# Attention block with a dense Mish layer: maxima ahead of the first scores in groups of three pairs, and other numbers of dense halves in the first and the last steps

## The chip, the core and the metric

The kernel runs on one core of a Trainium2 chip. Its engines are TensorE (PE in the profile; PEld is its weight load), VectorE (DVE), ScalarE (ACT), GpSimd (POOL) and SyncE (SP), which issues the transfers. Each has its own queue and works it off in order; semaphores tie them. The metric is the time of one execution on the device in microseconds (us). The median before is 1700.25 us, of three runs from 1697.17 to 1701.53.

## The reference

The input x is 2048 rows of 512. All arithmetic is float32.

```
mod = (silu(c) @ w_mod) -> six vectors sa, ca, ga, sb, cb, gb
h   = layernorm(x) * (1 + ca) + sa
q, k, v = h @ wqkv, 32 heads of 16
p   = softmax(q k^T / 4);  o = p v
x   = x + ga * (o @ wo)
h   = layernorm(x) * (1 + cb) + sb
u   = h @ w1 + b1                       (1792 columns)
x   = x + gb * ((u * tanh(softplus(u))) @ w2)
```

## The kernel before, in words

**Split numbers.** A dense product is made of three: each operand is split into a rounded high part and a remainder (wh and wl, h_h and h_l, a_h and a_l), and high times high, high times low and low times high are added in one PSUM bank.

**Attention, tiled.** There are 32 iterations n: four blocks of 512 queries by eight groups of four heads. An iteration has 16 steps, one for each 128 keys, so T = 512 steps t. The four heads of a group are two pairs j of two heads s. The tiles `ka` and `qa` hold a pair: one head in rows 0 to 63, the other in rows 64 to 127. A product of one head uses 64 of TensorE's 128 rows, so two products on different halves of the rows run at the same time.

The softmax needs each query's maximum before its scores are made, since the maximum is put as two more rows into `qa`, and the score comes out with it subtracted. So the scores are made twice. Once as *maxima* (`max_tile`: 128 queries by 512 keys in one bank, then VectorE's reduce to one column, L471 and L473), 64 for a pair of heads and 128 for an iteration, 20 steps ahead of the scores (PRO = 20). `neg_max` (L482) reduces them over the key blocks into `mm`, and `max_rows` transposes this to rows (L490), makes their high and low part `mh` and `mt` (L494, L495) and has SyncE put `mt` into `qa` (L501). The second time as *scores*, transposed (128 keys by 512 queries, L512), from which ScalarE makes the exponential `pr` (L520). The *values' product* `pv(t - 2)` (L540) then adds `vg` times `pr` into a bank over the 16 steps; `vg` is loaded for each iteration (L458).

**The banks.** Six of the eight PSUM banks are a ring. A maximum or a score takes the next bank, so each waits until what was there six banks earlier has been read; `ring(2)` takes two neighbours. The other two banks, `ms` and `acc`, take a dense accumulation and the values' product.

**A step from 0 on.** It has four scores, four maxima for the step 20 later (none in the last 20 steps), a values' product, and beside them f *halves* of the dense part: a dense matmul over 64 of its 128 rows, which runs beside a score or a maximum on the other 64. An even step has the halves of the upper rows, the odd step after it those of the lower rows of the same matmuls (`next_part`). f is 8 at most, and 3 in the last 20 steps. [...]

```
            if i < f:
                last = i + 1 == f
...
                if last:
...
                    cur["want"] = True
                    if i < len(mine) and mine[i]:
                        emit(mine[i])
```

`emit` notes the exponential of the next score as `cur["after"]`. With no maxima a step's scores have four slots, i = 0 to 3.

**The prologue.** Steps -20 to -1 have no scores. Each makes four maxima, and then `whole_units` works off whole dense matmuls (all 128 rows), in units of one bank, up to a credit of 7.5, where one is a matmul of 512 columns: 15 matmuls of 256 columns, or 8 of 512. These are the products of the later slices of wqkv (L126), in the order of `plan`; when a unit ends, its results go to memory (`qscr`, `kscr`, `vscr`), from where the pairs are loaded.

**What sets the order.** The program is written out in this order by `step`, and each engine keeps it. `hooks` run at fixed half-steps (2t and 2t + 1): loads, puts, and later stages of a unit. A unit begins when its `ready` time has come. The tail after step T (`tail`) makes the last block's output projection, the down products of the block before that were held, and the last block's dense layer.

Of the kernel before, what the change touches and what calls it, by code (L numbers as in the profile page):

```python
# [8 lines left out]
F32 = mybir.dt.float32  # L9
F32R = mybir.dt.float32r  # L10
AF = mybir.ActivationFunctionType
ALU = mybir.AluOpType
AX = mybir.AxisListType
# [5 lines left out]
def adaln_block(ctx: ExitStack, tc: tile.TileContext, x, wqkv, wo, w1, b1, w2, c, w_mod, out):  # L19
# [20 lines left out]
    CUT1, CUT2 = (0, 1), (2, 3)  # L40
    LOV = ((1,), (), (1, 3), (1, 3))
    PREP = 4
    CREDIT = 7.5
    HCAP = 10.0

    x = x[0]
# [416 lines left out]
    def max_tile(n, j, s, qs, kb):  # L463

        if n not in mxs:
            mxs[n] = ap.tile([P, 2, 8, 4], F32, tag="mx", name="mx", bufs=2)

        def product():
            kt, qt = ka[(2 * n + j) % NR], qa[(2 * n + j) % NR]
            pm = ring()  # L470
            nc.tensor.matmul(pm, qt[64 * s:64 * s + 64, qs * P:(qs + 1) * P], kt[64 * s:64 * s + 64, kb * TB:(kb + 1) * TB],  # L471
                             start=True, stop=True)
            return nc.vector.tensor_reduce(out=mxs[n][:, s, 4 * j + qs, kb:kb + 1], in_=pm, op=ALU.max, axis=AX.X)  # L473

        return product

    def neg_max(n):

        mx = mxs.pop(n)
        mm = ap.tile([P, 4, 2, 4], F32, tag="mm", name="mm", bufs=2)  # L480
        twice = bass.AP(tensor=mx.tensor, offset=mx.offset, ap=[list(mx.ap)[0], [16, 4], [0, 2], [4, 4], [1, 4]])
        nc.vector.tensor_reduce(out=mm, in_=twice, op=ALU.max, axis=AX.X)  # L482
        ats.setdefault(16 * n + 16 - PRO, []).append(lambda: max_rows(n, mm))
# [607 lines left out]
    def queue(ready, make):  # L1091
        units.append((ready, make))
# [4 lines left out]
    def next_part(h):  # L1097

        if not cur["left"] and units and h >= units[0][0]():
            cur["h"] = h  # L1100
            cur["fin"] = units.pop(0)[1]("ms")
            cur["left"], cur["first"] = list(pe_queue), True
            cur.pop("after", None)
            pe_queue.clear()
        slots = []
        for m in cur["left"]:
            if slots and len(slots[-1]) < 2 and m[0].shape[-1] <= TB // 2:
                slots[-1].append(m)
            else:
                slots.append([m])  # L1110
        n = len(slots)
        k = n if n <= 8 else (n + 1) // 2
        if h >= 2 * (T - PRO):
            k = 3
        cur["part"], cur["left"] = slots[:k], [m for l in slots[k:] for m in l]

    def whole_units(h, credit):

        while credit > 0:
            if not cur["left"]:  # L1120
                if not units or h < units[0][0]():
                    return
                cur["tag"] = "acc" if cur.get("tag") == "ms" else "ms"
                cur["h"] = h
                cur["fin"] = units.pop(0)[1](cur["tag"])
                cur["left"] = list(pe_queue)
                pe_queue.clear()
            m = cur["left"].pop(0)
            cur["first"] = False
            mm_go(m)  # L1130
            credit -= m[0].shape[-1] / TB
            if not cur["left"]:
                at(h + 1, lambda fin=cur["fin"]: fin(h + 1))
                cur["fin"] = None
# [7 lines left out]
    def step(t):  # L1142
        second = t % 2
        n, u = t // 16, t % 16 // 2
        tm = t + PRO
        run_hooks(2 * t)
        if t < 0:

            for i in range(2):
                if tm < 16:  # L1150
                    kb, jq = divmod(2 * tm + i, 8)
                else:
                    jq, kb = tm % 16 // 2, 2 * second + i
                for s in range(2):
                    max_tile(tm // 16, jq // 4, s, jq % 4, kb)()
            if second and tm % 16 == 15:
                neg_max(tm // 16)
            run_hooks(2 * t + 1)
            for f in ats.pop(t, []):
                f()  # L1160
            whole_units(2 * t + 1, CREDIT)
            do_specials(2 * t + 1)
            return
        s = 0 if second else 1
        own, others = ([score(n, j, v, 2 * u + i) for i in range(2) for j in range(2)] for v in (s, 1 - s))
        if not second and 1 < t < T:
            next_part(2 * t)
        part = list(cur["part"])
        f = len(part)
        if t >= T:  # L1170
            if t == T:
                cur["tag"] = "acc"
            run_hooks(2 * t + 1)
            pv(t - 2)
            whole_units(2 * t + 1, 8)
            do_specials(2 * t + 1)
            return
        swap, held = False, None
        if tm < T:
            o = max(0, (8 - f) // 2)  # L1180
            mo, alone = maxima(tm // 16, tm % 16 // 2, s, o)

            mine = [x for p in zip(mo, own) for x in p] + own[len(mo):]
            kinds = [k for p in zip("m" * len(mo), "s" * len(mo)) for k in p] + ["s"] * (len(own) - len(mo))
            swap = 2 <= f <= len(mine) and kinds[f - 1] == "s" and kinds[f - 2] == "m"
            if swap:
                mine[f - 2:f] = mine[f - 1], mine[f - 2]
        else:
            o = max(0, (4 - f) // 2)
            mine = own[o:] if second else own[:4 - o]  # L1190
            alone = others[4 - o:] if second else others[:o]

            m = len(mine)
            if f > m:
                mine = [mine[(i * m) // f] if (i + 1) * m // f > i * m // f else None for i in range(f)]
        beside = part + alone

        def emit(product):
            e = product()
            if cur.pop("want", None):  # L1200
                cur["after"] = e

        ends = second and f and not cur["left"]
        for i in range(max(len(mine), len(beside))):
            if i == len(mine) // 2:
                run_hooks(2 * t + 1)
            if i < f:
                last = i + 1 == f
                if i < len(mine) and mine[i] and not last:
                    if swap and ends and i + 2 == f:  # L1210
                        held = mine[i](True)
                    else:
                        emit(mine[i])
                for m in beside[i]:
                    mm_half(m, second, cur["first"], bool(ends and last and m is beside[i][-1]),
                            cur.pop("after", None))
                    cur["first"] = False
                if last:
                    if ends:
                        cur["fin"](2 * t + 2)  # L1220
                        cur["fin"] = None
                    if held:
                        held()
# [3 lines that stand above are left out]
            else:  # L1227
                for x in (*mine[i:i + 1], *beside[i:i + 1]):
                    emit(x)
        if tm < T and tm % 16 == 15:  # L1230
            neg_max(tm // 16)
        do_specials(2 * t + 1)
        pv(t - 2)
        for f in ats.pop(t, []):
            f()
# [13 lines left out]
    def planned(i, a, tag):  # L1249
        _, kind, sl, args = plan[i]  # L1250
        unit = v_unit(sl, a, tag) if kind == 2 else qk_unit(kind, sl, a, tag)

        def fin(h):
            if a == args[-1]:
                if i + 2 < len(plan):
                    d = (7 if i > 6 else 4) if h > 0 else 1
                    at(h + d, lambda: slice_split(*plan[i + 2][1:3]))
                    split_at[i + 2] = h + d
                if i + 3 < len(plan):
                    at(h + (9 if i > 6 else 7 if h > 0 else 2), lambda: slice_load(*plan[i + 3][1:3]))  # L1260
            unit(h)
            if (kind, sl, a) == (2, 0, NKC - 1):
                at(max(0, h + 2), lambda: first_mods(max(0, h + 2)))
            if i + 1 == len(plan) and a == args[-1]:
                mst["qkv"] = h // 2 + 3
        return fin
# [23 lines left out]
        queue_mod(j)  # L1290
    for i, (t0, _, _, args) in enumerate(plan):
        for a in args:
            queue(lambda i=i, t=t0: max(2 * t, split_at.get(i, 4 * T) + 4), lambda tag, i=i, a=a: planned(i, a, tag))

    preps = [(w1scr[f], w1[:, f * P:(f + 1) * P].rearrange("(k p) m -> p k m", p=P), None) for f in range(FT)]
    preps += [(woscr[k], wo[k * P:(k + 1) * P, :], 0) for k in range(DK)]
# [35 lines left out]
    def run_hooks(h):  # L1332
        while h in hooks:
            for f in hooks.pop(h):
                f()
# [37 lines left out]
```

## Time and profile before

| | before |
|---|---|
| median of three runs | 1700.25 us |
| the profiled execution | 1693.26 us |
| its span, first to last instruction | 1691.5 us |
| mean granted clock of TensorE | 0.996 |
| TensorE busy | 1660.6 us, 98% |
| VectorE busy | 1429.9 us, 85% |
| ScalarE busy | 1327.1 us, 78% |
| GpSimd busy | 898.0 us, 53% |
| VectorE's maxima L473, x2048 | 1276.1 us, 684 ns each |
| ScalarE's exponentials L520, x2048 | 1090.2 us, 605 ns each |

Times in the profile are in us from the first instruction, those of one instruction in a group in ns. The chain of waits is the work that ended last, followed back from the end; a row of it is a start, a length, an engine and a line. A timeline row groups instructions of one kind that follow each other, so a group of four matmuls at 0.73 is four that overlap. A matmul's end is modelled, so the distance of two starts tells more than a length.

### The profile page before, as it was taken

The numbers are of one execution on the slowest core, as the hardware profiler recorded it, in microseconds if no ns is written. First come the engines' busy times: TensorE is split into PE (matmuls) and PEld (weight loads), VectorE is DVE, ScalarE is ACT, GpSimd is POOL, SyncE is SP. The second block draws the span as 40 slices with busy tenths as digits, with TensorE's granted clock in tenths as the row PEclk, the third lists the DMA queues.
The fourth block names the chain that finished last, engine by engine and source line by source line (L and its number), as shares of the span: only waits on it lengthen the run. The fifth ranks groups of instructions, "written<-read, shape, count | busy, mean of one in ns | idle before, by whom it ended". The sixth has DMA issues, their size and how long they took to land.

```text
span 1691.5 us, 32962 instructions
## 1 busy us (share of the span) xinstructions
PE 1660.6 (98%) x12316; PEld 921.7 (54%) x12316; DVE 1429.9 (85%) x2362; ACT 1327.1 (78%) x2559; POOL 898.0 (53%) x906
## 2 busy tenths in 40 slices
PE   6999999999999999999999999999999999999998
PEld 5755665554435455555555555555555555554687
DVE  6898898887998888988888888889888888881577
ACT  6247777777778898888889898888888898889264
POOL 5155215565504388755525498654535597646432
PEclk9999999999999999999999999999999999999999
DMA  7767457777772342434353644334442535332362
GB/s 249 192 224 215 120 159 213 250 226 226 232 210 63 111 123 74 127 80 149 86 133 74 197 105 99 99 109 123 117 103 79 176 95 131 93 107 82 132 218 74
DMA packets 113992, 240.03 MB, mean 142 GB/s; under 512 B 24048, under 2 KB 49648, under 8 KB 107784
## 3 DMA queue, kind: packets, MB, share of 16 engines
q1 hardware_dynamic: 113832, 237.92, 49.6%
q8 instruction: 97, 1.59, 0.4%
q14 instruction: 63, 0.52, 0.1%
HBM read 179.95 MB, written 51.44 MB: 137 GB/s over the span
## 4 chain that ended last, share of the span: by engine, by line
PE 92%; DVE 3%; DMA 2%; ACT 2%; SPq 1%; issue 1%; POOL 0%; DVEq 0%; ACTq 0%; POOLq 0%
PE bk L540 30%; PE ring L471 23%; PE ring L512 22%; PE bk L132 9%; PE bk L126 3%; PE ring L126 3%; PE ring L1074 2%; DVE mx L473 1%; ACT pr L520 1%; DMA xt<-in_A_x 1%; SPq L318 0%; DMA qa<-mt 0%; PE bk L1006 0%; DMA vg<-vscr 0%; PE ring L842 0%
## 5 line engine op out<-in xcount | busy, mean ns | idle before, releaser
L473 DVE TENSOR_REDUCE mx<-ring 128x1 f32<-128x512 f32 x2048 | 1276.1, 684 | 161.5 <-PE bk L132 104.9
L520 ACT ACTIVATE pr<-ring 128x512 f32<-128x512 f32 x2048 | 1090.2, 605 | 232.0 <-PE bk L132 168.8
L471 PE MATMUL ring<-ka,qa 64*128 64x512 f32 x2048 | 778.7, 427 | 0.5
L512 PE MATMUL ring<-qa,ka 64*128 64x512 f32 x2048 | 723.0, 397 | 7.8 <-ACT pr L520 4.6
L471 PEld LDWEIGHTS ring<-ka,qa 64*128 64x128 f32 x2048 | 366.5, 184 | 407.9 <-DVE mx L473 356.2
L540 PE MATMUL bk<-pr,vg 128*32 128x512 f32 x4096 | 545.9, 605 | 0.0
L512 PEld LDWEIGHTS ring<-qa,ka 64*128 64x128 f32 x2048 | 374.1, 184 | 120.8 <-ACT pr L520 35.6
L132 PE MATMUL bk<-h,w 64*128 64x512 f32 x1008 | 280.7, 410 | 0.0
L132 PE MATMUL bk<-w,a_h 64*128 64x512 f32 x576 | 194.8, 417 | 0.6 <-ACT pr L520 0.4
L132 PEld LDWEIGHTS bk<-h,w 64*128 64x128 f32 x1008 | 171.5, 184 | 5.7 <-ACT pr L520 0.4
L540 PEld LDWEIGHTS bk<-pr,vg 128*32 128x32 f32 x4096 | 81.0, 108 | 125.1 <-issue 117.0
L740 POOL TENSOR_SCALAR ee<-hb 128x512 f32<-128x512 f32 x42 | 62.5, 1488 | 96.7 <-ACT hb L734 88.2
L132 PE MATMUL bk<-w,a_l 64*128 64x512 f32 x288 | 113.7, 395 | 0.0
L770 POOL TENSOR_TENSOR ee<-ee,rr 128x512 f32<-128x512 f32 x42 | 53.9, 1284 | 111.6 <-ACT rr L761 111.4
L132 PEld LDWEIGHTS bk<-w,a_h 64*128 64x128 f32 x576 | 95.3, 185 | 5.2 <-ACT pr L520 1.5
L132 PE MATMUL bk<-w,o_hl 64*128 64x512 f32 x288 | 79.7, 409 | 0.0
L98 POOL TENSOR_TENSOR a_l<-hb,a_h 128x512 fp32r<-128x512 f32 x53 | 71.7, 1354 | 4.4
L893 POOL TENSOR_TENSOR y<-yd,y 128x512 f32<-128x512 f32 x40 | 51.4, 1285 | 35.5 <-ACT yd L892 35.3
L754 POOL TENSOR_SCALAR rr<-ee 128x512 f32<-128x512 f32 x42 | 26.1, 622 | 60.0 <-ACT ee L746 59.9
L132 PE MATMUL bk<-h_h,wl 64*128 64x512 f32 x168 | 57.5, 423 | 0.0
L95 POOL TENSOR_SCALAR a_h<-hb 128x512 fp32r<-128x512 f32 x53 | 36.3, 684 | 39.9 <-DVE hb L768 38.3
L774 POOL TENSOR_TENSOR hb<-hb,rr 128x512 f32<-128x512 f32 x42 | 54.5, 1298 | 3.3
(205 smaller groups left out, 1840.9 us busy)
## 6 DMA issues: line engine op xcount, KB each, us to landing
ka<-kscr SPq DMA_DIRECT2D x124, 384.0 KB
w<-w2scr SPq DMA_DIRECT2D x56, 512.0 KB
w<-w1scr SPq DMA_DIRECT2D x46, 512.0 KB
vg<-vscr SPq DMA_DIRECT2D x32, 552.0 KB
qa<-qscr SPq DMA_DIRECT2D x124, 100.0 KB
kscr<-qh SPq DMA_DIRECT2D x16, 512.0 KB
qscr<-qh SPq DMA_DIRECT2D x32, 256.0 KB
hl<-in_B_w SPq DMA_DIRECT2D x28, 256.0 KB
```

Source lines behind the costliest of these rows:

```text
L98: (nc.gpsimd if eng == "p" else nc.vector).tensor_sub(lo, src, hi.bitcast(F32))
L126: nc.tensor.matmul(acc, l, r, start=start, stop=stop)
L132: i = nc.tensor.matmul(acc, l[64 * g:64 * g + 64], r[64 * g:64 * g + 64], start=start, stop=stop)
L471: nc.tensor.matmul(pm, qt[64 * s:64 * s + 64, qs * P:(qs + 1) * P], kt[64 * s:64 * s + 64, kb * TB:(kb + 1) * TB], start=True, stop=True)
L473: return nc.vector.tensor_reduce(out=mxs[n][:, s, 4 * j + qs, kb:kb + 1], in_=pm, op=ALU.max, axis=AX.X)
L512: nc.tensor.matmul(p_, kt[64 * s:64 * s + 64, kc * P:(kc + 1) * P], qt[64 * s:64 * s + 64, :], start=True, stop=True)
L520: e = nc.scalar.activation(pr, p_, AF.Exp, scale=SCALE)
L540: nc.tensor.matmul(accs[n][32 * h:32 * h + 32, :], vgs[n][:, o:o + 32], pts.pop((t, h)), start=(kc == 0), stop=(kc == 15))
L740: nc.gpsimd.tensor_scalar_min(buf("ee", 2), b["hb"], HCAP)
L770: nc.gpsimd.tensor_mul(ee, ee, rr)
L774: nc.gpsimd.tensor_mul(hb, hb, rr)
L893: nc.gpsimd.tensor_add(y[i], yd, y[i])
```

## The change

**Prologue.** The maxima are made in groups of three pairs. A pair is the two heads' product for the same queries and keys; `max_pair` writes both into two neighbouring banks of the ring and reduces both with one instruction, 128x2 out of 128x2x512. A group stands in every third half-step, followed by whole dense matmuls up to a credit of 3 x 3.6 = 10.8: 22 of 256 columns or 11 of 512. Forty pairs are thirteen groups and one pair alone, which has a credit of 1. `neg_max(0)` stands right after pair 31 and `max_rows(0)` after pairs 33 to 35, ahead of the dense matmuls of that step. The prologue has four dense matmuls of 512 columns fewer than before, and the steps from 0 on have them as eight halves.

**First steps.** The halves begin with step 0 instead of step 2: f was 0, 0, 8, 8, 6, 6 and so on, and is 6 from step 0 on.

**Last 20 steps.** The largest number of halves is 4 instead of 3. f was 3 in each; it is 4, 4, 2, 2, then twelve times 4, then four times 0. The first half of a step after one with f = 4 waits for the exponential of the fourth score.

**Split slices.** A unit whose weight slice is split in the prologue may begin one half-step after the split rather than four.

From step 4 to step 491 TensorE, VectorE, ScalarE and GpSimd have the same instructions in the same order.

```diff
-    CREDIT = 7.5
+    CREDIT = 3.6
...
+    def max_pair(n, j, qs, kb):
+
+        if n not in mxs:
+            mxs[n] = ap.tile([P, 2, 8, 4], F32, tag="mx", name="mx", bufs=2)
+        kt, qt = ka[(2 * n + j) % NR], qa[(2 * n + j) % NR]
+        pm = ring(2)
+        for s in range(2):
+            nc.tensor.matmul(pm[:, s, :], qt[64 * s:64 * s + 64, qs * P:(qs + 1) * P],
+                             kt[64 * s:64 * s + 64, kb * TB:(kb + 1) * TB], start=True, stop=True)
+        nc.vector.tensor_reduce(out=mxs[n][:, :, 4 * j + qs, kb], in_=pm, op=ALU.max, axis=AX.X)
...
         if h >= 2 * (T - PRO):
-            k = 3
+            k = 4
...
         if t < 0:
 
             for i in range(2):
-                if tm < 16:
-                    kb, jq = divmod(2 * tm + i, 8)
-                else:
-                    jq, kb = tm % 16 // 2, 2 * second + i
-                for s in range(2):
-                    max_tile(tm // 16, jq // 4, s, jq % 4, kb)()
-            if second and tm % 16 == 15:
-                neg_max(tm // 16)
-            run_hooks(2 * t + 1)
-            for f in ats.pop(t, []):
-                f()
-            whole_units(2 * t + 1, CREDIT)
+                run_hooks(2 * t + i)
+                pairs = [p for p in range(2 * tm + i, min(2 * tm + i + 3, 2 * PRO)) if (2 * tm + i) % 3 == 0]
+                for p in pairs:
+                    kb, jq = divmod(p, 8) if p < 32 else (p % 4, p % 32 // 4)
+                    max_pair(p // 32, jq // 4, jq % 4, kb)
+                    if p % 32 == 31:
+                        neg_max(p // 32)
+                if i:
+                    for f in ats.pop(t, []):
+                        f()
+                if pairs:
+                    whole_units(2 * t + i, 3 * CREDIT if len(pairs) == 3 else 1)
             do_specials(2 * t + 1)
             return
...
-        if not second and 1 < t < T:
+        if not second and t < T:
             next_part(2 * t)
...
-            queue(lambda i=i, t=t0: max(2 * t, split_at.get(i, 4 * T) + 4), lambda tag, i=i, a=a: planned(i, a, tag))
+            queue(lambda i=i, t=t0: max(2 * t, split_at.get(i, 4 * T) + (4 if split_at.get(i, 0) > 0 else 1)), lambda tag, i=i, a=a: planned(i, a, tag))
```

The order that comes of it is shown at four places. A row has the line, the operation, out<-in and the shape. Lines from L477 on are 11 higher after the change.

TensorE in the prologue, from one set of maxima to the next. Before:

```order
L471 MATMUL ring<-ka_104,qa_106 128x512 x4
L126 MATMUL bk<-wh,h_h 128x256 x4
L126 MATMUL bk<-wl,h_h 128x256 x4
L126 MATMUL bk<-wh,h_l 128x256 x4
L126 MATMUL bk<-wh,h_h 128x256 x3
L471 MATMUL ring<-ka_104,qa_106 128x512 x4
```

And after:

```order
L484 MATMUL ring<-ka_104,qa_106 128x512 x6
L126 MATMUL bk<-wh,h_h 128x256 x4
L126 MATMUL bk<-wl,h_h 128x256 x4
L126 MATMUL bk<-wh,h_l 128x256 x4
L126 MATMUL bk<-wh,h_h 128x256 x4
L126 MATMUL bk<-wl,h_h 128x256 x4
L126 MATMUL bk<-wh,h_l 128x256 x2
L484 MATMUL ring<-ka_104,qa_106 128x512 x2
L484 MATMUL ring<-ka_105,qa_107 128x512 x4
```

Four maxima to 15 dense matmuls became six to 22.

VectorE's queue of maxima over the prologue and into the first steps. Before:

```order
L473 TENSOR_REDUCE mx<-ring 128x1 x64
L482 TENSOR_REDUCE mm<-mx 128x32
L473 TENSOR_REDUCE mx<-ring 128x1 x4
L494 TENSOR_SCALAR mh<-ring 32x128
L495 SCALAR_TENSOR_TENSOR mt<-mh,lows,ring 32x128
L473 TENSOR_REDUCE mx<-ring 128x1 x60
```

And after:

```order
L486 TENSOR_REDUCE mx<-ring 128x2 x32
L493 TENSOR_REDUCE mm<-mx 128x32
L486 TENSOR_REDUCE mx<-ring 128x2 x4
L505 TENSOR_SCALAR mh<-ring 32x128
L506 SCALAR_TENSOR_TENSOR mt<-mh,lows,ring 32x128
L486 TENSOR_REDUCE mx<-ring 128x2 x4
L473 TENSOR_REDUCE mx<-ring 128x1 x48
```

Sixty-four reduces of a bank became thirty-two of two banks; between mm and mh stand four pairs (eight banks) instead of four banks.

SyncE's queue around the puts of the maxima's rows into `qa` (`wr` is a raw slice of wqkv, `ql` and `qh` are the parts of a finished q or k unit). Before:

```order
L501 DMA qa_106<-mt 2x4x128 x2
L501 DMA qa_107<-mt 2x4x128 x2
L458 DMA vg<-vscr 128x1104
L214 DMA wr<-in_A_wqkv 128x4x256
L252 DMA qscr<-ql 8x16x512
L252 DMA qscr<-qh 8x16x512 x2
```

And after:

```order
L512 DMA qa_106<-mt 2x4x128 x2
L512 DMA qa_107<-mt 2x4x128 x2
L214 DMA wr<-in_A_wqkv 128x4x256
L252 DMA qscr<-ql 8x16x512
L252 DMA qscr<-qh 8x16x512 x2
L458 DMA vg<-vscr 128x1104
```

The load of `vg` moved behind the load of `wr` and three puts.

TensorE in the last 20 steps, one step, with the wait that stands on a dense half (`Activation_49` is ScalarE's semaphore). Before:

```order
L512 MATMUL ring<-qa_108,ka_633 128x512
L132 MATMUL bk<-w_16036,a_h 128x512 [waits Activation_49]
L512 MATMUL ring<-qa_109,ka_634 128x512
L132 MATMUL bk<-w_16036,a_h 128x512
L132 MATMUL bk<-w_16036,a_l 128x512
L512 MATMUL ring<-qa_108,ka_633 128x512
L512 MATMUL ring<-qa_109,ka_634 128x512
L540 MATMUL bk<-pr_2_1177,vg 32x512
```

And after:

```order
L523 MATMUL ring<-qa_108,ka_633 128x512
L132 MATMUL bk<-w_16861,a_l 128x512 [waits Activation_49]
L523 MATMUL ring<-qa_109,ka_634 128x512
L132 MATMUL bk<-w_16896,a_h 128x512
L523 MATMUL ring<-qa_108,ka_633 128x512
L132 MATMUL bk<-w_16896,a_h 128x512
L132 MATMUL bk<-w_16896,a_l 128x512
L523 MATMUL ring<-qa_109,ka_634 128x512
L551 MATMUL bk<-pr_0_1140,vg 32x512
```

A fourth half stands ahead of the fourth score, and the wait of the next step's first half is on that score's exponential.

## The prediction

> **What bounds the kernel now.** I read the page first (its span, engines, chain by engine, costliest groups), then the chain of waits at both ends of the program, since the change leaves the middle as it is, then the timelines there.
>
> ```profile
> span 1691.5 us, 32962 instructions
> PE 1660.6 (98%) x12316; PEld 921.7 (54%) x12316; DVE 1429.9 (85%) x2362; ACT 1327.1 (78%) x2559; POOL 898.0 (53%) x906
> PE 92%; DVE 3%; DMA 2%; ACT 2%; SPq 1%; issue 1%; POOL 0%; DVEq 0%; ACTq 0%; POOLq 0%
> L473 DVE TENSOR_REDUCE mx<-ring 128x1 f32<-128x512 f32 x2048 | 1276.1, 684 | 161.5 <-PE bk L132 104.9
> ```
>
> TensorE carries 92% of the chain, VectorE 3%, ScalarE 2%. From step 4 to step 491 the four compute engines have the same work in the same order in both programs, so I take no difference there. What is left is about 60 us at the start and 45 us at the end. The chain at the start (start, duration, what):
>
> ```profile
> 50.16 0.66 PE ring L471 x3
> ...
> 53.88 1.08 PE ring L471 x4
> ...
> 56.94 0.66 PE ring L471 x4
> 57.61 1.99 PE bk L126 x15
> ...
> 80.85 0.66 PE ring L471 x4
> 81.51 2.04 PE bk L126 x8
> ...
> 91.67 0.47 PE ring L471 x2
> 92.14 2.48 DVE mx L473 x4
> 94.65 0.29 DVE mm L482
> ...
> 97.89 12.57 DVE mx L473 x21
> 110.50 0.50 PE ring L512
> ...
> 111.23 1.00 PE bk L540 x8
> ...
> 114.43 1.00 PE bk L540 x8
> ...
> 117.26 0.99 PE bk L540 x8
> ```
>
> Until 91.67 it is TensorE alone: a prologue step is four maxima (0.66) and then whole dense matmuls, 1.99 for fifteen of 256 columns or 2.04 for eight of 512, so 2.65 or 2.70. From 92.14 to 110.5 VectorE is the chain: its maxima, back to back at 12.57/21 = 0.60, are late, and the first scores stand in the same ring of banks behind them. From 111.23 it is TensorE again.
>
> The first two steps took 3.72 and 3.06; 1.48 over two of 2.65. The row of that stretch has a granted clock of 0.66 (the number ahead of the DMA share), and 1.00 in the next stretches, so I leave these 1.48 as they are:
>
> ```profile
> 50.00:55.00 5.00, 5.00 (x25) 3.75 (x25) 3.44 (x6) 1.48 (x3) 1.28 (x1) 0.66 0.58 205
> ```
>
> **The prologue's new price.** The parts, from the timeline:
>
> ```profile
> 58.36 0.64 PE L126 MATMUL bk<-wh,h_h 128*128 128x256 f32 x4
> 78.08 0.73 PE L471 MATMUL ring<-ka,qa 64*128 64x512 f32 x4
> 78.61 2.48 DVE L473 TENSOR_REDUCE mx<-ring 128x1 f32<-128x512 f32 x4
> 79.08 1.09 PE L126 MATMUL bk<-h_h,wl 128*128 128x512 f32 x4
> ```
>
> A 256-column matmul starts every 0.12 (2.0 for fifteen, with 0.19 for the first), a 512-column one every 0.23 (2.04 = 8 x 0.23 + 0.20), a maximum of a head every 0.115 after the first ((0.73 - 0.39)/3, a lone one taking 0.39), since two heads run on the two halves of the rows. A reduce starts 0.53 after its matmuls do and takes 0.62.
>
> After the change, a group of three pairs on TensorE is 0.66 + 2 x 0.115 = 0.89, then 22 matmuls of 256 (22 x 0.12 + 0.19 = 2.83) or 11 of 512 (11 x 0.23 + 0.20 = 2.73): 3.72 or 3.62, where one and a half steps were 3.98 or 4.05. Pairs 0 to 29 are ten groups; the 144 narrow matmuls fill 6.5 of them, so 6.5 x 3.72 + 3.5 x 3.62 = 36.9. The group that holds pairs 30 to 32 starts at 50.16 + 1.48 + 36.9 = 88.5; before, pairs 30 and 31 started at 91.67. That is 3.2 us gained, if VectorE keeps up.
>
> The reduce of a pair, 128x2x512, is not in the trace. Its lower bound: the single at 0.60 plus 512 more elements at the slope between the single (684 ns mean, 512 elements) and mm (0.29, 128 elements), (684-290)/384 = 1.03 ns each, 0.53: 1.13. Upper bound: two of the group's mean, 1.37; two back to back are 1.20 to 1.24. I take 1.14, nearest to the slope, since the fixed part should be paid once. Three are then 3.42, under the 3.62 of a group, and TensorE stays the bound. [...]
>
> After the groups, VectorE's order decides. Reduce of pair 30 from 89.0, 31 to 91.3, mm 0.29 (94.65 row), 32 to 92.7, 33 to 93.9. The transposes of the maxima need pair 33's two banks (the ring of six is full), so TensorE, with the dense matmuls queued behind them, stands still for about 1.1 until 93.9. Pairs 34 and 35 to 96.1, mh and mt about 0.6 to 96.7; pairs 36 to 38 from 97.2 to 100.65, the last pair to 102.0. Then nine singles of 0.60, the last nine of the 21 in the 12.57 row, to 107.4, where before it was 110.46: 3.0 gained. The halves that now stand in steps 0 and 1 lie under these reduces (a step of four singles is 2.4; TensorE's part of such a step without the values' product is 2.83 - 1.00 = 1.8). Step 3 has six halves instead of eight: 114.43 - 111.23 = 3.20 becomes 117.26 - 114.43 = 2.83, 0.37 gained. Fewer instructions on VectorE (40 fewer) are worth nothing elsewhere.
>
> SyncE's queue: the four puts of the maxima's rows now come two loads and three puts earlier than the load of vg.
>
> ```profile
> 99.23 3.07 SPq L501 DMA_DIRECT2D qa<-mt  x4
> 102.35 0.39 SPq L458 DMA_DIRECT2D vg<-vscr  x1
> ...
> 104.48 1.55 SPq L252 DMA_DIRECT2D qscr<-qh  x2
> ```
> ```profile
> 104.30 0.50 PE L512 MATMUL ring<-qa,ka 64*128 64x512 f32 x1
> ```
>
> The rows took 104.30 - 102.30 = 2.0 at most from the last issue to the first score. After the change mt is ready near 96.7 and the puts end near 100.3 or earlier, so the first score can start by 102.3, when TensorE arrives at about 101.5; VectorE has its backlog until 102.0 and on, which covers that. The vg load, before at 102.35, goes behind the qscr puts, in the times of before to 104.48 + 1.55 - 0.39 = 105.6; with mt about 2 us earlier I put it at 103.6. Its first reader, the values' product (111.23 before), now wants it at 108.2. Before, its landing was hidden in 8.9 us; now 4.6 are left. The nearest transfer I can see, the rows' 2.0, fits; vg is larger, so I add 0.2. Prologue: -3.0 - 0.37 + 0.2 = **-3.2**; with the pair reduce at 1.24 it is -2, and if the standstill of 1.1 goes too, -4.5.
>
> **The end.** Without maxima a step is four scores, four exponentials, three halves (now four, for fourteen of the steps) and a values' product.
>
> ```profile
> 1526.64 0.50 PE L512 MATMUL ring<-qa,ka 64*128 64x512 f32 x1
> ...
> 1549.24 0.50 PE L512 MATMUL ring<-qa,ka 64*128 64x512 f32 x1
> 1549.29 0.50 PE L132 MATMUL bk<-w,a_h 64*128 64x512 f32 x1
> ...
> 1551.36 0.50 PE L512 MATMUL ring<-qa,ka 64*128 64x512 f32 x1
> 1551.92 0.49 PE L132 MATMUL bk<-w,a_h 64*128 64x512 f32 x1
> ...
> 1553.81 0.49 PE L512 MATMUL ring<-qa,ka 64*128 64x512 f32 x1
> ...
> 1569.77 2.78 PE L540 MATMUL bk<-pr,vg 128*32 128x512 f32 x24
> ```
> ```profile
> 1549.77 1.08 ACT pr L520 x2
> 1550.86 0.52 ACT rr L761
> 1551.38 0.50 ACT pr L520
> ```
> ```profile
> 1555.79 15.45 ACT L520 ACTIVATE pr<-ring 128x512 f32<-128x512 f32 x29
> ```
>
> The first two steps shown are an ordinary one (1549.24 to 1551.36, 2.12) and one that waits (to 1553.81, 2.45). The wait is on a rule in the code: a step's first half is held until the exponential of the score written at the last slot of the step before has ended. With three halves that is the third exponential. It starts 0.53 after the step's first score (1549.77 - 1549.24) at the earliest, each takes 15.45/29 = 0.53 (0.52 where ACT is pressed), so the third ends at 0.53 + 1.58 = 2.11, and the next step's half is due at 2.12 + 0.05 = 2.17: no wait, unless ScalarE has one more operation between, as at 1550.86; then the half starts 0.04 after the third exponential (1551.92) and the next step 1.89 later (1553.81).
>
> With four halves the last slot's score is the fourth, whose exponential ends at 0.53 + 2.10 = 2.63. The half is held from 2.17 to 2.67, the next three scores stand behind it in TensorE's order, and the step that starts after it comes 1.89 + 0.23 (the fourth half, in a row of halves that nothing hides now) = 2.12 later, at 4.79. By then ScalarE has just ended that step's exponentials and starts anew: two steps take 4.7 to 4.8 instead of 4.24, 0.46 to 0.55 more, and there are seven such pairs: 3.2 to 3.9. I walked all twenty steps by these durations with the extra ScalarE operations in their places. The walk of before gives 43.6 to 43.9 for 44.13 in the trace (1526.64 to 1569.77 + 1.0) and its long steps; that of after ends its last exponential 3.7 later. One exponential of the last mish unit (0.5) that stood behind the last score now stands ahead of six; it is in that walk. Before, three products of values (2.78) end the stretch; now one or two are left, 0.3 back. **+3.3.** The bounds: +0.3 if the held half never costs anything, +5 if ScalarE's extra operations all add to it.
>
> Nothing comes back for the dense part's earlier end:
>
> ```profile
> 1584.65 1.29 POOL L98 TENSOR_TENSOR a_l<-hb,a_h 128x512 fp32r<-128x512 f32 x1
> ...
> 1598.62 0.71 PE L126 MATMUL ring<-w,a_h 128*128 128x512 f32 x2
> ```
>
> The last unit's output is ready at 1585.9, and the tail's products on the later blocks run from 1598.62; the units it feeds come after. The four last steps have no halves, but ScalarE's four exponentials still take 2.1 each.
>
> **Sum.** -3.2 + 3.3 = +0.1. The profiled execution took 1693.26 (span 1691.5), under the 1700.25 that is the median of the runs; I carry the difference over to the median: 1700.4.
>
> **The rivals.** (B) The held half costs little, because the order on the chip lets ScalarE run ahead: then 1700.25 - 3.2 + 0.3 = 1697.3, and with the prologue's better bound 1696.1; with an end that gains its 0.3 and more from the dense part's early finish it is under 1695. For it: an ordinary step of three halves has no wait; against it: the step at 1551.36, which waits in just this way. (C) Slower: the pair reduce costs two of the mean, 1.37. Then three are 4.11, VectorE is the bound of each group (4.11 against 3.7, ten groups: +4) and pairs 30 to 39 cost 0.23 more each (+2.3): 1700.4 + 6 = 1706.4. It decides from 1.33 on, where the sum passes 0.3%. Against it: the back-to-back singles of 0.60. (D) The values' product waits for vg: it decides at 4.6 us from issue to landing, and the worst, the 8.9 that the trace allows, gives 1700.4 + 4.3 = 1704.7. (E) The pair reduce costs two singles back to back, 2.48/2 = 1.24: three take 3.72, TensorE and VectorE run level in each group, and pairs 30 to 39 cost 0.10 more each: 1701.4. [...] That the change does less than it says (the pairs not back to back) is within C and E.
>
> **How the numbers follow.** Two runs of this kernel tell about 0.3% apart, 5.1 us: 1695.2 to 1705.3. Both parts cancelling, 1697 to 1704: 0.50. B 0.17, of which most with something more gained at the end, under 1695.2. C with other ways for the prologue to lose 0.15, D 0.10, E 0.08. The two ends of D's and A's range put a few hundredths over the line. Faster 0.19, same 0.55, slower 0.26. The range takes B's and C's nearer halves: 1694.5 to 1706.5.
>
> **What would show it.** In the profile after: groups of 0.89 and 22 or 11 dense matmuls every 3.6 to 3.7 until about 88.5; the pair reduce at 1.14, three in a row without idle TensorE; the first values' product near 108; from 1523 on steps alternating 2.1 and 2.6; the last exponential within 0.5 us of 1571.2 (1555.79 + 15.45). A pair reduce over 1.25, a stop of TensorE before its first values' product, or last steps all of 2.12, would make it wrong.

## The result and the profile after

The changed kernel takes 1708.03 us (median of 7 runs, 1704.15 to 1710.56), the kernel before 1697.32 (7 runs, 1691.92 to 1701.53): slower by a ratio of 1.0061, 95% interval 1.0047 to 1.0075. That is 10.7 us by the medians, 0.6%, and 1.5 us over the predicted range. The page of the changed kernel begins:

```profile
span 1708.8 us, 32922 instructions
```

The reduce to `mm` is done once an iteration, after its 64 maxima (2048 in 32 iterations; the 128 named with the kernel is wrong), at the same place in both programs, and so serves as a milestone. Its timeline rows after (first, second and last of 32; start, duration):

```profile
93.67 0.29 DVE L493 TENSOR_REDUCE mm<-mx 128x32 f32<-128x128 f32 x1
147.81 0.29 DVE L493 TENSOR_REDUCE mm<-mx 128x32 f32<-128x128 f32 x1
1541.73 0.29 DVE L493 TENSOR_REDUCE mm<-mx 128x32 f32<-128x128 f32 x1
```

and the second and the last of before:

```profile
139.70 0.29 DVE L482 TENSOR_REDUCE mm<-mx 128x32 f32<-128x128 f32 x1
1526.88 0.29 DVE L482 TENSOR_REDUCE mm<-mx 128x32 f32<-128x128 f32 x1
```

The first stands 1.0 us earlier than before (94.65), the second 8.1 later, the last 14.9 later, the end of the span 17.3 later. So 9.1 us are lost between 94 and 148 us, 2.4 behind the last milestone, and 6.7 in the middle. Of the middle's, 5.1 are in TensorE's waits for the maxima's rows of later iterations, from 130 to 1600 us (total, times, longest); after:

```profile
PE ring L523 <- DMA qa<-mt: 7.6, 3, 4.2
```

and before:

```profile
PE ring L512 <- DMA qa<-mt: 2.5, 1, 2.5
```

These waits differ between profiles whose middle has the same work: 4.7 in one of the kernel before with only its last 20 steps changed (e5 below), 4.0 in one with the groups of three (e6). The profile of before is also a low one of its kernel, 1693.26 for a median of 1697, and that of the changed kernel the longest of its seven, 1710.56. So the two profiles differ by more than the medians; start and end, 8.1 + 2.4 = 10.5, are about the size of the 10.7.

**The start.** The chain after, in the prologue:

```profile
52.24 4.99 PE bk L126 x22
...
61.35 0.89 PE ring L484 x6
62.24 2.83 PE bk L126 x22
65.07 0.89 PE ring L484 x6
...
83.53 0.90 PE ring L484 x6
...
87.13 0.94 PE ring L484 x6
...
90.81 0.94 PE ring L484 x6
```

The groups run as reckoned, 0.89 and 2.83, 3.72 in all (61.35 to 65.07), later 3.60. But pair 30's group starts at 90.81, 2.3 later than forecast. SyncE's queue and TensorE's timeline around the first scores (a number in brackets is idle time and what ended it):

```profile
95.32 0.80 SPq L303 DMA_DIRECT2D ka<-kscr  x2
98.25 0.39 SPq L214 DMA_DIRECT2D wr<-in_A_wqkv  x1
...
99.77 2.98 SPq L512 DMA_DIRECT2D qa<-mt  x4
105.82 0.39 SPq L214 DMA_DIRECT2D wr<-in_A_wqkv  x1
...
108.43 1.64 SPq L458 DMA_DIRECT2D vg<-vscr  x1
```
```profile
105.93 0.79 PE L523 MATMUL ring<-qa,ka 64*128 64x512 f32 x1 [1.82 <-DMA qa<-mt]
...
116.91 1.94 PE L551 MATMUL bk<-pr,vg 128*32 128x512 f32 x8 [3.32 <-DMA vg<-vscr]
...
122.06 1.47 PE L551 MATMUL bk<-pr,vg 128*32 128x512 f32 x8
```

The first score waits 1.82 us for the maxima's rows, issued only 0.5 us later than before (99.77 against 99.23). The first values' product waits 3.32 us for vg: 108.43 is 6.1 later than before, because the wr load ahead of it could not be issued before wr was free, at 105.82, and it then took 8.5 us to the product. What held wr is in the chain: the slice in it landed 5.50 us after its issue, and only then could ScalarE and GpSimd split it, until 105.80 (start, length):

```profile
98.25 5.50 DMA wr<-in_A_wqkv
...
104.53 1.27 POOL wl L98
```

Behind each stop the granted clock (the number ahead of the DMA share) is low, 0.66 and then 0.61 and 0.71:

```profile
105.00:110.00 5.00, 4.07 (x19) 2.94 (x21) 2.34 (x5) 2.48 (x6) 2.66 (x3) 0.66 0.50 145
...
115.00:120.00 5.00, 3.09 (x14) 1.24 (x16) 0.39 (x1) 0.00 (x0) 1.63 (x1) 0.61 0.92 332
120.00:125.00 5.00, 5.00 (x32) 2.65 (x30) 3.29 (x6) 3.55 (x7) 4.76 (x5) 0.71 0.07 28
```

So the product of the second step starts 122.06 - 116.91 = 5.15 after the first, where before it was 114.43 - 111.23 = 3.20. Of the 8.1 us, 5.7 stand at the first values' product (116.91 against 111.23) and nearly all of the rest by the second.

**The end.** TensorE's and ScalarE's timelines in two of the last steps:

```profile
1571.50 0.49 PE L523 MATMUL ring<-qa,ka 64*128 64x512 f32 x1
...
1573.67 0.50 PE L523 MATMUL ring<-qa,ka 64*128 64x512 f32 x1
1574.14 0.49 PE L132 MATMUL bk<-h,w 64*128 64x512 f32 x1
...
1576.26 0.49 PE L523 MATMUL ring<-qa,ka 64*128 64x512 f32 x1
...
1587.05 4.07 PE L551 MATMUL bk<-pr,vg 128*32 128x512 f32 x24
```
```profile
1572.03 4.24 ACT L531 ACTIVATE pr<-ring 128x512 f32<-128x512 f32 x8 [0.53 <-PE ring L523]
```

One step (1571.50 to 1573.67) waits for nothing and takes 2.17, the next holds its half for 0.47 and takes 2.59: 4.76 for two instead of 4.24. ScalarE, which should be the bound here, idles 0.53 us in every eight exponentials. From the last `mm` to the end of the last values' products it is 45.7 us before (1526.88 to 1569.77 + 2.78) and 49.4 after (1541.73 to 1587.05 + 4.07), 3.7 more. The end of the span shows only 2.4 because 1.3 come back in the tail: both traces have a stop of TensorE of 2.42 us there (until 1604.08 and 1622.64), behind which the granted clock is 0.72 before (1605 to 1610) and 1.00 after (1620 to 1630). The tail behind the products takes 119.0 us in before and in e3, which has four halves, and 117.7 in the changed kernel and in e5, so this is a difference of executions, not of the change.

### The profile page after: what moved, and what is told of

Read it like the earlier page. It is cut to its first block, busy times and chain, and to the rows that moved or that the text cites. A ratio compares the mean times of both kernels' runs of the same rounds, so it can differ in the third digit from the quotient of the medians.

```text
span 1708.8 us, 32922 instructions
## 1 busy us (share of the span) xinstructions
PE 1665.0 (97%) x12320; PEld 924.8 (54%) x12320; DVE 1427.1 (84%) x2322; ACT 1326.7 (78%) x2559; POOL 897.5 (53%) x906
## 3 DMA queue, kind: packets, MB, share of 16 engines
q1 hardware_dynamic: 113832, 237.92, 49.4%
## 4 chain that ended last, share of the span: by engine, by line
PE 89%; DMA 3%; ACT 2%; DVE 2%; POOL 2%; issue 1%; SPq 0%; DVEq 0%; POOLq 0%; ACTq 0%
PE bk L551 29%; PE ring L471 22%; PE ring L523 21%; PE bk L132 9%; PE bk L126 3%; PE ring L126 2%; ACT pr L531 2%; PE ring L1085 2%; DMA qa<-mt 1%; PE ring L484 1%; DMA wma<-in_w_mod 1%; DVE mx L473 0%; DMA wm<-in_w_mod 0%; POOL wm L634 0%; DVE hf L374 0%
## 5 line engine op out<-in xcount | busy, mean ns | idle before, releaser
L473 DVE TENSOR_REDUCE mx<-ring 128x1 f32<-128x512 f32 x1968 | 1227.4, 684 | 174.3 <-PE bk L132 119.6
L471 PE MATMUL ring<-ka,qa 64*128 64x512 f32 x1968 | 764.4, 427 | 0.0
L471 PEld LDWEIGHTS ring<-ka,qa 64*128 64x128 f32 x1968 | 361.6, 185 | 402.8 <-DVE mx L473 350.9
L98 POOL TENSOR_TENSOR wl<-wr,wh 128x512 fp32r<-128x512 f32 (+1 forms) x13 | 17.7, 1365 | 75.9 <-ACT wh L91 43.6
```

The costliest lines, as they stand in the source:

```text
L98: (nc.gpsimd if eng == "p" else nc.vector).tensor_sub(lo, src, hi.bitcast(F32))
```

## The experiments

The theories: A, the held half costs the end 2 to 4 us; B, vg and the rows of the maxima are late because of their places in SyncE's queue; against B, C, the transfers of 95 to 115 us are too many in any order. A median is given with that of before from runs made beside it; a ratio is to before, with its 95% interval.

**e1, three halves again.**

```diff
         if h >= 2 * (T - PRO):
-            k = 4
+            k = 3
```

> The changed kernel with three halves in each of the last 20 steps again, nothing else undone. The traces put +8.1 us on the start and +2.4 on the end (the offset of the second reduce to mm is 8.1, that of the span 17.3, of which 14.8 stand ahead of the last 20 steps). Theory A, the held half of a step costs the end 2.4 to 3.3: this kernel is 2.4 to 3.3 us faster than the changed kernel, about 8 us slower than before, and its last 20 steps are 2.12 each again. Rival, the end's difference is only carried over from the start: the same time as the changed kernel, within 0.5 us.

Measured: 1704.24 us, before 1697.41, ratio 1.0045 (1.0029 to 1.0061). The difference to before falls from 10.7 to 6.8 us, by 3.9; the intervals of the two kernels overlap, so it is the profile, and e5 below, that decide. A holds for the end: its last steps run without a wait, and the offset to before stays the same from the last milestone on (10.7 there, 10.6 at the span's end). The first scores and the first values' product wait as in the changed kernel.

**e2, vg back at its place.**

```diff
-    at(-3, lambda: load_v(0))
+    at(-4, lambda: load_v(0))
```

> The changed kernel with the load of vg directly behind the maxima's rows, where it stood before; the other transfers keep the new order. Theory B, the place of vg in SyncE's queue costs the 3.75 us for which TensorE waited for it and the lower granted clock after that stop: the first values' product has no wait for vg, starts near 113.5 instead of 116.9, and the time falls by 5 to 6 us to about 1702. Rival C, the transfers of 95 to 115 us are too many for the DMA engines in whatever order: the product still waits for vg, or the first scores wait longer for the rows, and less than 2 us are won.

Measured: 1703.62 us, before 1697.41, ratio 1.0043 (1.0022 to 1.0065); 4.5 us of the 10.7 are gone by the medians, though the two intervals overlap. vg is not waited for, but in the profiled execution the first scores wait longer for their rows:

```profile
108.37 0.79 PE L523 MATMUL ring<-qa,ka 64*128 64x512 f32 x1 [5.02 <-DMA qa<-mt]
...
116.64 1.06 PE L551 MATMUL bk<-pr,vg 128*32 128x512 f32 x8
```

So vg's place is worth most of what B expected, and part of C is seen: the product came no earlier (116.64), only the stop and the low clock behind it are gone (1.00 over 115 to 120 us, in the changed kernel 0.61).

**e3, vg and the load of the fourth pair back.** As e2, and

```diff
-    for pp, h in ((2, -22), (3, -8)):
+    for pp, h in ((2, -22), (3, -10)):
```

> As the kernel with vg back, and the load of the fourth pair of q and k ahead of the last kscr puts, where it stood before: SyncE's queue is that of before around the first scores. Theory B with the fourth pair's 0.9 MB in the way of the maxima's rows: the rows land 2 us after their issue instead of 3.2, the first scores start near 104 instead of 105.9, and the time falls by 7 to 8 us to about 1700, with the end's 2.4 left over. Rival, the rows are late because mt is late (four pair reduces between mm and mh instead of four single ones, mt at 99.0 against 97.9): the first scores still wait 1 us or more, and it is within 1 us of the kernel with vg back alone.

Measured: 1698.95 us, before 1697.41, ratio 1.0013 (1.0003 to 1.0024). Another 4.7 us are gone, as B expected, and within 1.5 us of before although the end still has four halves. The first score still waits, but shorter, and the values' product starts at 111.86:

```profile
105.11 0.50 PE L523 MATMUL ring<-qa,ka 64*128 64x512 f32 x1 [1.65 <-DMA qa<-mt]
...
111.86 1.07 PE L551 MATMUL bk<-pr,vg 128*32 128x512 f32 x8
```

**e4, the kernel before with vg late.**

```diff
-    at(-3, lambda: load_v(0))
+    at(-1, lambda: load_v(0))
```

> The kernel before with the load of vg behind the load of wr and the three qscr puts, as in the changed kernel; nothing else. It prices that place alone. Theory B: vg is issued near 106.0, lands 6 to 8 us later, the first values' product moves from 111.2 to about 113 or 114, the granted clock falls after the stop, and the kernel is 3 to 6 us slower than before. Rival, vg is late in the changed kernel only because its queue waited for a free wr: issued at 106.0 it is there by 111.2 and the time is that of before within 1 us.

Measured: 1703.13 us, before 1697.41, ratio 1.0039 (1.0024 to 1.0053): this place alone costs 5.7 us. SyncE's row and TensorE's:

```profile
109.47 1.29 SPq L458 DMA_DIRECT2D vg<-vscr  x1
```
```profile
117.68 1.94 PE L540 MATMUL bk<-pr,vg 128*32 128x512 f32 x8 [5.15 <-DMA vg<-vscr]
```

The rival falls: vg needs 8.2 us from its issue, and was issued 3.5 us later than I put it, since the wr loads ahead of it waited for their buffers here too (the first went out at 100.27, 2.6 later than before, with mt only 0.1 later).

**e5, the kernel before with four halves.**

```diff
-            k = 3
+            k = 4
```

> The kernel before with four halves in a step of the last 20, the start untouched. Theory A: the end costs 2.4 to 3.9 us (2.4 by the spans of the two traces, 3.8 between the changed kernel and the one with three halves), so it is that much slower than before, and its last 20 steps alternate 2.1 and 2.6. Rival, the end costs this only behind a disturbed start: within 1 us of before.

Measured: 1700.33 us, before 1697.06, ratio 1.0024 (1.0012 to 1.0035), 3.3 us. A holds without a disturbed start: ScalarE's rows have the same gap,

```profile
1566.14 4.24 ACT L520 ACTIVATE pr<-ring 128x512 f32<-128x512 f32 x8 [0.54 <-PE ring L512]
```

**e6, SyncE's order of before and three halves.** e3 and e1 together; of the change there remain the groups of three pairs, the halves from step 0 and the earlier unit after a split.

> The changed kernel with SyncE's order of before (vg and the fourth pair back) and three halves in the last 20 steps: what is left are the groups of three pairs and the halves from step 0. The kernel with SyncE's order back was 1.5 us slower than before, 2.4 to 3.9 of it the end's: so 1 to 2.4 us faster than before. Rival, the groups themselves gain nothing, since the rows of the maxima come no earlier (mt behind four pair reduces) and the first scores wait for them: the time of before within 0.5 us.

Measured: 1696.28 us, before 1697.06, ratio 0.9998 (0.9986 to 1.0009). No difference: the rival. Where the groups' gain goes is seen against the profile of e5, whose start is that of before. e6, then e5 (first maxima, where the first group stops, first values' product):

```profile
52.08 0.97 PE L484 MATMUL ring<-ka,qa 64*128 64x512 f32 x5
53.59 0.49 PE L484 MATMUL ring<-ka,qa 64*128 64x512 f32 x1 [0.54 <-DVE ql L98]
54.01 0.75 PE L126 MATMUL bk<-wh,h_h 128*128 128x256 f32 x4
...
104.76 0.49 PE L523 MATMUL ring<-qa,ka 64*128 64x512 f32 x1 [1.38 <-DMA qa<-mt]
...
111.41 1.06 PE L551 MATMUL bk<-pr,vg 128*32 128x512 f32 x8
```
```profile
49.85 0.73 PE L471 MATMUL ring<-ka,qa 64*128 64x512 f32 x4
50.52 0.75 PE L126 MATMUL bk<-wh,h_h 128*128 128x256 f32 x4
...
110.30 1.07 PE L540 MATMUL bk<-pr,vg 128*32 128x512 f32 x8
```

The first group takes 54.01 - 52.08 = 1.93 to its dense matmuls instead of 0.89: it needs all six banks, and the sixth is held by a set-up unit until VectorE has made its ql. (The later start itself, 52.08 against 49.85, stands ahead of the first maximum.) The product comes 59.33 us after the first maximum, in e5 60.45. So 1.1 us of the forecast 3.2 are left there in these two profiles; 1.0 went at the first group and 1.4 in the wait for the rows. Even the 1.1 is no more than starts differ by: in e8, whose maxima are those of before, the product comes 59.60 after the first. SyncE had mt's puts behind a wr load that went out at 99.79, 1.5 after mt.

**e7, the rows ahead of wr.** As e6, with the puts of the first rows right behind mt and the wr load behind them.

```diff
-        at(2 * (16 * n + 16 - PRO) + 3, put)
+        put() if n == 0 else at(2 * (16 * n + 16 - PRO) + 3, put)
...
-                    at(h + (9 if i > 6 else 7 if h > 0 else 2), lambda: slice_load(*plan[i + 3][1:3]))
+                    x = h + (9 if i > 6 else 7 if h > 0 else 2)
+                    at(-6 if -10 < x < -4 else x, lambda: slice_load(*plan[i + 3][1:3]))
```

> As the kernel with SyncE's order of before and three halves, but the four puts of the first maxima's rows go straight behind mt, ahead of the load of wr, which in the profiles held SyncE until wr was free (100.15 with the order back) while mt was ready. Theory D, the first scores wait because the rows' puts stand behind a load that waits for its buffer: the wait of 1.65 us is gone and it is 1 to 2 us faster than the kernel with the order back. Rival, the rows are late by the transfers that run at the time, or mt is: no change within 0.7 us, or a loss, where the later wr delays the weights of the next dense unit.

Measured: 1699.66 us, before 1697.06, ratio 1.0017 (1.0003 to 1.0031). The wait for the rows is gone from the profile, and the values' product starts at 113.24, later than in e6. The rival holds, by another way than it says: wr now comes later, ScalarE stands still for it with the first exponentials behind that in its queue (they start at 106.67, in e6 at 105.29), and TensorE waits 1.08 us for them. Behind that its scores and maxima start 0.43 us apart (109.01, 109.44, 109.87), later 0.23 (117.40, 117.63, 117.86). ScalarE, then TensorE:

```profile
105.66 0.62 ACT L91 CAST wh<-wr 128x512 fp32r<-128x512 f32 x1 [4.58 <-DMA wr<-in_A_wqkv]
...
106.67 3.67 ACT L531 ACTIVATE pr<-ring 128x512 f32<-128x512 f32 x7
```
```profile
104.51 0.39 PE L523 MATMUL ring<-qa,ka 64*128 64x512 f32 x1
...
113.24 1.07 PE L551 MATMUL bk<-pr,vg 128*32 128x512 f32 x8
```

**e8, the kernel before with the rows ahead of wr.** The first edit of e7 in before.

> The kernel before with only the puts of the first maxima's rows moved ahead of the load of wr and one unit's kscr puts. In the profile of before the first scores did not wait for the rows, in that of the same kernel with a late vg they waited 1.2 us. Theory D: 0 to 1.5 us faster than before, according to how often the wait occurs. Rival: the rows' early transfer changes nothing, within 0.5 us.

Measured: 1698.88 us, before 1697.06, ratio 1.0010 (0.9994 to 1.0026). Nothing won.

**e9 and e12, two pairs in the first group.** As e6, with groups of 2, twelve times 3, and 2 pairs.

```diff
-                pairs = [p for p in range(2 * tm + i, min(2 * tm + i + 3, 2 * PRO)) if (2 * tm + i) % 3 == 0]
+                q = 2 * tm + i
+                pairs = list(range(q, min(q + 3, 2 * PRO))) if q % 3 == 2 else [0, 1] if q == 0 else []
...
-                    whole_units(2 * t + i, 3 * CREDIT if len(pairs) == 3 else 1)
+                    whole_units(2 * t + i, len(pairs) * CREDIT if q < 38 else 4.6)
```

> As the kernel with SyncE's order of before and three halves (0.8 us under before), but the groups of pairs are 2, then twelve of 3, then 2. In the profiles the first group of three needs all six banks of the ring, one of which a set-up unit holds until VectorE has made its ql: the sixth maximum stops TensorE (0.54 us idle, 2.2 from the group's start to its dense matmuls instead of 0.9). And mt stands behind four pair reduces, with these groups behind three. Theory E: the stop at the start is gone (1.0 to 1.3 us), mt comes another 1.2 us earlier, the first scores wait less for their rows: 1.5 to 3 us faster than the kernel with three in the first group, so 2 to 4 us faster than before. Rival: what is won at the start the first scores give back, because their rows land when the transfers of 95 to 105 us let them: within 0.7 us of the kernel with three.

> The kernel with two pairs in the first group once more, beside the one with early puts: 1.7 us under before as in the run before, give or take 1.5.

Measured: 1694.81 us, before 1696.50, ratio 0.9991 (0.9979 to 1.0004); once more 1697.00, before 1696.48, ratio 0.9997 (0.9985 to 1.0009). The first group's stop is gone, and mt is ready at 95.52, in e6 at 98.28 (1.8 of these 2.8 us stand ahead of the first maximum, 50.31 here). The rows are put only 0.4 earlier, and the first score waits 1.44:

```profile
95.18 0.34 DVE L506 SCALAR_TENSOR_TENSOR mt<-mh,lows,ring 32x128 fp32r<-32x128 f32 x1
```
```profile
99.39 0.38 SPq L214 DMA_DIRECT2D wr<-in_A_wqkv  x1
...
100.90 3.02 SPq L512 DMA_DIRECT2D qa<-mt  x4
```

Theory E falls by the time. What VectorE and TensorE win ahead of the rows ends at SyncE, which issues the puts 5.4 us after mt, behind a wr load that waits for its buffer. TensorE also stops for 1.52 us, until 99.41 (1.07 in e12, 1.66 in e11), for the low part of a weight slice that GpSimd makes from wr.

**e11, both.** e9 with the first edit of e7.

> As the kernel with two pairs in the first group, but the first maxima's rows are put into qa straight behind mt. In the profile of that kernel mt was ready at 95.5 and its puts were issued from 100.9, behind a wr load that SyncE could issue only at 99.4; the first scores waited 1.4 us for the rows. Theory D: the wait goes, 1 to 1.4 us faster than with the late puts. Rival, as in the two runs that put the rows first before (2.6 and 1.8 us over before): wr and vg come later by as much, and the time is the same or up to 3 us longer.

Measured: 1697.24 us, before 1696.48, ratio 0.9998 (0.9985 to 1.0011). The rows go out at 99.43, the first score at 105.19 waits for none, and the values' product starts at 112.33, against 110.97 in e9; from the first maximum it is 60.24 against 60.66, so most of the wait won is lost again (TensorE waits 0.74 us for ScalarE's exponentials, as in e7). No version of the groups was clearly faster than before.

**e10, the loads behind vg later.** The changed kernel, with the two wm loads that follow vg ten half-steps later.

```diff
-                at(max(0, h + 2), lambda: first_mods(max(0, h + 2)))
+                at(max(0, h + 2) + 10, lambda: first_mods(max(0, h + 2) + 10))
```

> The changed kernel with the loads of w_mod's slices (wm, 0.5 MB each), which follow vg at once in SyncE's queue, ten half-steps later; they shift what follows them in the middle of the program, so the time is only to be read at the start. In the changed kernel vg was issued at 108.4 to 110.1 and waited for until 116.9. Theory B, the place in the queue: vg comes at most 1 us earlier. Rival C, the wm transfers slow vg: it lands 2 to 4 us earlier, and the first values' product starts by 114.5.

Measured: 1709.70 us (two runs), before 1696.50, ratio 1.0073 (1.0044 to 1.0102). vg was issued at 110.17 and its reader started at 119.65, 9.5 us later, so vg is slow without the wm loads right behind it:

```profile
119.65 1.31 PE L551 MATMUL bk<-pr,vg 128*32 128x512 f32 x8 [3.25 <-DMA vg<-vscr]
```

This bears on the cause as well. In the changed kernel the chain from 98 to 151 us runs through wr, SyncE, a wm load (110.12, 8.18 us) and GpSimd's work on it, not through vg; here, with wm later, it runs through wr and vg. Both stand behind the same wr load.

## Why the prediction was wrong

**Where the 10.7 us come from**, taken off one after the other: vg's place 4.5 (e2; alone in before 5.7, e4), the fourth pair's place 4.7 (e3), the fourth half 2.3 (e6 against e3; 3.9 and 3.3 in e1 and e5). By the ratios it is 3.1, 5.1 and 2.5. Clear of noise are the two loads together (e3), vg's place alone (e4) and the fourth half alone (e5); how the 9.2 divide between the loads is not. Then 0.8 under before is left, which can't be told from nothing. The sum was -3.2 + 3.3; measured, the end is near +3.3, and the start +7 to +8.

**The step that failed** is the one on SyncE's queue. "Before, its landing was hidden in 8.9 us; now 4.6 are left. The nearest transfer I can see, the rows' 2.0, fits": vg takes 7.8 to 9.5 us to its reader wherever it was waited for (e1, e4, the changed kernel, e10), about four times the row I took it from; at its old place it landed within 7.0 (e9, e12, which do not wait for it). I put its issue at 103.6 by moving the queue's rows with mt, 2 us earlier, where my own rows give 1.2 (96.7 against 97.89); mt came at 99.04, later than before. The issue was at 108.43: the wr load ahead of it, the only load there and not one of two, waits until GpSimd is done with wr, which does not move with mt. This was rival D, with a chance of 0.10 and a worst price of 4.3; alone it costs 5.7, with the low clock behind the stop (0.72 and 0.60 over 115 to 125 us in e4).

**The second thing missed in that queue** is the fourth pair's load. The prediction has no term for it, though the order of SyncE was there to be read: its q and k, about 1 MB, went out at 89.2 to 91.3 before, and from 94.09 to 96.12 now, just ahead of wr and the rows. Its k parts before:

```profile
90.54 0.80 SPq L303 DMA_DIRECT2D ka<-kscr  x2
```

The sentence that the rows need 2.0 us and lie under VectorE's backlog fell with it: 1.82 us of wait after, and none in the profile of before. e3 shows that the two loads together are 9.2 us. What the pair's load does shows in the transfers behind it. With it late (the changed kernel, e1, e2, e10), the first score starts 6.2 to 8.1 us after the rows' first put, and wr lands 5.5 to 7.4 after its issue. With it at its old place, the rows take 3.5 to 3.9 (e3, e4, e6, e9, e12, all of which wait for them) and wr 3.0 to 3.6 (before, e3 to e6, e12). In the changed kernel vg stands behind wr, so the pair's place can make it later too, and the 4.5 and the 4.7 need not be two separate costs.

**The groups.** The price of a pair reduce was right: three take 3.49, 1.16 each (1.14 forecast), so rivals C and E, 1.37 and 1.24 a pair, fall.

```profile
69.27 3.49 DVE L486 TENSOR_REDUCE mx<-ring 128x2 f32<-128x1024 f32 x3 [0.24 <-PE ring L484]
```

The trace has 1.22 for one reduce of a pair and 0.68 for one of a single bank; what counts here is the distance of two in a row, 1.16 and 0.60. The group's 3.72 and 3.60 were right as well. But -3.2 became -0.8, within the measurement's uncertainty: I had counted 0.89 for the first group, which takes 1.93, since the full ring has to be free, and I had taken what mt and the first scores gain as a gain of the whole, though SyncE's queue does not follow mt (e9: ready at 95.5, its puts from 100.9). Another 1.0 us in the changed kernel's own profile is the clock: 0.62 and 0.69 over 50 to 60 us (the 4.99 for 22 matmuls at 52.24), where before has 0.66 and 1.00. e1 has it too (0.60 and 0.72), e2 and e3 have 1.00, so it comes with the execution, not with the change.

**The end** was right: 4.76 for two steps (forecast 4.7 to 4.8), +2.3 to +3.9 by the runs (forecast 3.3). By the profiles it is 3.7, from the last `mm` to the end of the last values' products: 49.4 us with four halves (the changed kernel, e3, e5), 45.6 to 45.7 with three (before, e1, e6). The 0.3 that I took back for fewer products behind the last exponential did not come: three steps' products end the stretch (24 in 4.07 us, before 24 in 2.78). That nothing comes back for the dense part's earlier end was right; the 1.3 in the tail go with the granted clock there, 0.72 in before and 1.00 in the changed kernel.

**The chances.** Slower by over 0.3% had 0.26. The sign of the sum hung on the two covers in SyncE's queue, and I had bounded the landing by the row of a transfer that is far smaller.

## What to carry to other kernels

When an order changes, go through the transfer queue as through a compute engine: each load's issue is held by whatever stands ahead and waits for a buffer (vg went out at 108.43 instead of 102.35, behind a wr load issued at 105.82), and a large load put ahead of others can make them land later (wr in 5.5 to 7.4 us instead of 3.0 to 3.6). A load that nobody waits for (vg before) shows no landing time, and so no cover can be read from it. Bound an unknown landing by the longest allowance the trace shows, not by the shortest transfer. And when one engine gets earlier, ask which queue the result passes next: here the maxima's rows lay ready for 5.4 us behind a load that waited for its buffer, and moving them ahead of it only passed the delay to that load and its readers (e7, e11).

## What the runs showed of the hardware

A stop of TensorE can cost more than its length. In two profiles (after, e2) the granted clock was at 0.61 to 0.66 over the 5 us in which a stop of 1.8 us or more around the first scores ended, and the scores and maxima then started every 0.42 us instead of 0.23 (106.52, 106.94, 107.37 and later 109.63, 109.87, 110.10 in the changed kernel). The shortest of these is 1.82 (the changed kernel), and one of 1.96 us in e1 left 0.66 as well. After the stops of 1.38 and 1.65 us in e6 and e3 it stayed at 1.00. The length alone does not decide: the stop of 2.42 us in the tail left 0.72 in before and 1.00 in the changed kernel. What else decides, no run shows. The window of e2:

```profile
105.00:110.00 5.00, 1.63 (x8) 1.36 (x10) 0.38 (x1) 1.80 (x3) 3.05 (x3) 0.64 0.83 283
```
